# Larger first-batch loads and an earlier third weight product in a fused attention and SwiGLU kernel

## Chip, cores, metric

One core of one Trainium2 chip. The metric is the device time of one execution in microseconds; lower is better. A core's profile gives the span from its first to its last instruction, about 1.8 us less than the time.

## The reference

```python
def _attn_ref(q, k, v, tau):                       # q, k, v: (4, 6016, 256) float32, tau = 1
    qn = q / (np.linalg.norm(q, axis=1, keepdims=True) + 1e-06)
    kn = k / (np.linalg.norm(k, axis=1, keepdims=True) + 1e-06)
    s = kn.transpose(0, 2, 1) @ qn / tau           # 256 x 256 per batch
    s = s - s.max(-1, keepdims=True)
    a = np.exp(s)
    a /= a.sum(-1, keepdims=True) + 1e-09
    return (v @ a).astype(np.float32)

def _moe_ref(x, w_gate, w_val, w_out):             # x: 24064 rows of 256, hidden width 1536
    g = x @ w_gate
    silu = g * (1.0 / (1.0 + np.exp(-g)))
    val = x @ w_val
    return (silu * val @ w_out).astype(np.float32)
```

## The kernel before

The kernel folds the attention matrix into the gate and value weights (the "weight products", `Wg` and `Wv`) and then streams v through the two weighted stages. Batches 1 to 3 do their attention work behind the stream of the batch before. Batch 0 can't: its k and q (47 tiles of 128 rows each, loaded as float32 and cast to fp8 by the DMA) must arrive, be multiplied and normed before the stream starts. That prologue, the first 40 us of some 812, is what the change touches.

Load order and groups (four tiles a load, 4 KB a partition):

```python
groups = [(s, min(4, NS - s)) for s in range(0, NS, 4)]
...                                                            # cut
gs, gm = groups[-1]
qgroups = groups[:-1] + [(s, min(2, NS - s)) for s in range(gs, NS, 2)]
NQ = len(qgroups)
order = [(g, 1, groups) for g in range(NG)] + [(g, 0, qgroups) for g in range(NQ)]
for n, (g, which, gl) in enumerate(order):
    load_qk(0, g, which, gl)                                   # all on the GpSimd queue
    ...                                                        # cut: constants at n == 8
load_first_v()
load_w(0, HW); load_w(HW, WP)                                  # first weight block, in halves
load_v(*allc[1])
for wc in range(1, NWC):
    load_w(wc * WP, (wc + 1) * WP)                             # second weight block first
```

What each group sets off, and the tail:

```python
    sqs = [first_square(0, t, which, on_dve=(t % 2 == 1)) for t in ts]   # ACT and DVE
    if which == 0:
        for t in ts:
            gemm1_pair(0, t)                       # k-times-q products on TensorE, fp8
        if g == G_COLS:                            # from tile 36 on: column sums
            first_cols(0)
    ...                                            # cut: row or column sums of the squares
# tail, in first_softmax(0):
    row_eps(rs)
    transpose_first_v()                            # waits for the first v load
    keep_warm(3)                                   # three 128x512 matmuls on ones
    ...                                            # cut: exponentials on ACT, two halves
    row_sum(0)
    wp_matmul(b, 0, 0, units[0], lo)
    wp_matmul(b, 1, 0, units[1], lo)
    row_sum(1)
    finish_rs(b, rs)
    wp_matmul(b, 0, 1, units[0], lo)
    wp_matmul(b, 1, 1, units[1], lo)
    for u in (2, 3):
        for jh in range(CH):
            wp_matmul(b, u, jh, units[u], lo)
```

`keep_warm` was there before; its name says that it is meant for TensorE's granted clock, the share of its full rate that a throttle lets it run at.

## Time and profile before

| | before |
|---|---|
| time, first three runs | 813.64, 813.80, 814.92; median 813.80 us |
| span of the profiled execution | 811.9 us, mean granted clock 1.000 |
| TensorE busy | 98% of the span |
| first use of q's last tile | 34.37 us |
| TensorE takes over from the loads | 40.60 us |

A row of a timeline reads: start, length, engine, line, operation, output<-inputs, shape, count, and in brackets the idle time before it with what ended it. An engine's line "PEld" is TensorE's weight loads.

### The profile page before, as it was taken

Reading aid. Unit: us, or ns where it says so; the run is one execution under the profiler, and the core shown is the slowest. Engines: PE = TensorE matmul, PEld = TensorE weight load, DVE = VectorE, ACT = ScalarE, POOL = GpSimd, SP = SyncE. Lnnn points to the kernel's source line nnn. Section 1 sums busy time; section 2 is a strip of 40 time slices with the busy share of each in tenths; the row PEclk is TensorE's granted clock in tenths of the full one; section 3 lists DMA queues with packets and bytes.
Section 4 is the critical chain, followed back from the end, with each engine's and each line's share of the span. In section 5 each row is a group of like instructions: output and inputs, shape, how many; then the busy total and the mean of one; then the engine's idle time right before and its main releaser. Section 6 shows DMA issues by size and latency. Waiting matters only on the chain.

```text
span 811.9 us, 13668 instructions
## 1 busy us (share of the span) xinstructions
PE 794.1 (98%) x4952; PEld 488.9 (60%) x5042; DVE 524.3 (65%) x795; ACT 434.8 (54%) x757; POOL 267.2 (33%) x330
## 2 busy tenths in 40 slices
PE   5999999999999999999999999999999999999998
PEld 3656666665565666666565666666556565665666
DVE  4777777657556777656755677765765555555554
ACT  4666655545555556545555556654554544444543
POOL 5515887423000888722100488752300000000000
PEclk9999999999999999999999999999999999999999
DMA  9993875329312678334912377641942112112101
GB/s 87 142 157 69 115 105 86 80 34 150 77 40 46 96 100 106 74 65 95 127 40 59 53 96 112 89 78 37 171 102 66 46 50 55 52 40 65 50 27 59
DMA packets 93747, 64.99 MB, mean 80 GB/s; under 512 B 52896, under 2 KB 92448, under 8 KB 92928
## 3 DMA queue, kind: packets, MB, share of 16 engines
q0 software_dynamic: 19584, 27.41, 29.0%
q1 hardware_dynamic: 73952, 36.65, 18.2%
q8 instruction: 39, 0.64, 0.4%
q14 instruction: 28, 0.23, 0.1%
q10 hardware_dynamic: 144, 0.07, 0.0%
HBM read 79.04 MB, written 36.70 MB: 143 GB/s over the span
## 4 chain that ended last, share of the span: by engine, by line
PE 93%; DMA 4%; issue 1%; DVE 1%; POOL 0%; ACT 0%; POOLq 0%
PE o_new L457 30%; PE v_ps L423 30%; PE g_ps L423 28%; DMA q_sb<-in_q_dram 2%; PE ps L392 2%; PE kq_new L151 2%; DMA k_sb<-in_k_dram 1%; DMA w_gate_sb<-in_moe_w_gate_dram 1%; DVE sv L433 0%; POOL k_sb L106 0%; ACT silu L429 0%; PE last_ps L481 0%; POOL vb L114 0%; DVE sq L274 0%; PE kq_new L156 0%
## 5 line engine op out<-in xcount | busy, mean ns | idle before, releaser
L433 DVE TENSOR_TENSOR sv<-silu,v_ps 128x512 bf16<-128x512 bf16 (+1 forms) x576 | 388.3, 674 | 263.9 <-ACT silu L429 261.1
L429 ACT ACTIVATE silu<-g_ps 128x512 bf16<-128x512 f32 (+1 forms) x576 | 338.7, 588 | 323.4 <-PE g_ps L423 257.5
L457 PE MATMUL o_new<-w_out_sb,sv 128*128 128x256 bf16 x2244 | 337.2, 273 | 1.5
L423 PE MATMUL v_ps<-vT,Wv 128*128 128x512 bf16 (+1 forms) x1100 | 324.3, 374 | 2.9
L423 PE MATMUL g_ps<-vT,Wg 128*128 128x512 bf16 (+1 forms) x1074 | 319.1, 375 | 0.3
L457 PEld LDWEIGHTS <-sv 128*128 128x128 bf16 x2244 | 219.6, 98 | 140.6
L423 PEld LDWEIGHTS <-Wv 128*128 128x128 bf16 x1152 | 112.7, 98 | 130.7
L284 POOL TENSOR_TENSOR acc_new<-acc_new,sq 128x512 f32<-128x512 f32 x135 | 157.6, 1167 | 45.1 <-DVE sq L274 36.9
L423 PEld LDWEIGHTS <-Wg 128*128 128x128 bf16 x1152 | 109.7, 98 | 24.9
L274 DVE TENSOR_TENSOR sq<-q_sb 128x512 bf16<-128x512 fp8e5 x72 | 65.9, 915 | 0.0
L279 POOL TENSOR_TENSOR acc_new<-sq 128x512 f32<-128x512 bf16 x3 | 3.5, 1154 | 150.5 <-DVE sq L274 150.5
L275 ACT ACTIVATE sq<-k_sb 128x512 bf16<-128x512 fp8e5 x72 | 44.2, 614 | 0.0
L466 ACT COPY o_sb<-o_new 128x512 f32<-128x512 f32 x48 | 28.1, 586 | 14.9 <-PE o_new L457 14.5
L151 PE MATMUL kq_new<-k_sb,q_sb 128*128 128x512 fp8e5 x184 | 32.0, 295 | 0.5 <-DMA q_sb<-in_q_dram 0.5
L106 POOL DMA_DIRECT2D q_sb<-in_q_dram x49 | 27.4, 558 | 13.5 <-DMA k_sb<-in_k_dram 5.5
L468 DVE COPY o_sb<-o_new 128x512 f32<-128x512 f32 (+1 forms) x47 | 31.3, 666 | 0.0
L106 POOL DMA_DIRECT2D k_sb<-in_k_dram x48 | 26.0, 542 | 10.4 <-DMA w_out_sb<-in_moe_w_out_dram 5.6
L178 PE MATMUL ss_new<-sq,ones_bf 128*128 128x256 bf16 x83 | 17.8, 353 | 9.1 <-ACT sq L168 8.6
L114 POOL DMA_DIRECT2D vb<-in_v_dram x47 | 24.1, 515 | 5.3 <-DMA vb<-in_v_dram 4.1
L151 PEld LDWEIGHTS <-q_sb 128*128 128x256 fp8e5 x184 | 21.2, 138 | 2.6 <-DMA q_sb<-in_q_dram 2.0
L178 PEld LDWEIGHTS <-ones_bf 128*128 128x128 bf16 x83 | 9.9, 122 | 15.9 <-issue 11.6
L312 POOL TENSOR_TENSOR inv<-inv,half 128x4 f32<-128x4 f32 x3 | 3.1, 1036 | 36.7 <-DVE inv L311 36.7
(94 smaller groups left out, 195.9 us busy)
## 6 DMA issues: line engine op xcount, KB each, us to landing
out_dram<-o_sb SPq DMA_DIRECT2D x92, 256.0 KB, 2.5
vb<-in_v_dram POOLq DMA_DIRECT2D x43, 256.0 KB, 5.9
k_sb<-in_k_dram POOLq DMA_DIRECT2D x44, 128.0 KB, 5.9
q_sb<-in_q_dram POOLq DMA_DIRECT2D x44, 128.0 KB, 5.1
w_out_sb<-in_moe_w_out_dram POOLq DMA_DIRECT2D x1, 768.0 KB, 13.7
vb<-in_v_dram POOLq DMA_DIRECT2D x4, 192.0 KB, 3.5
vT<-vb SPq DMA_TRANSPOSE x47, 4.3
w_gate_sb<-in_moe_w_gate_dram POOLq DMA_DIRECT2D x2, 256.0 KB, 7.0
```

Source lines behind the costliest of these rows:

```text
L106: nc.gpsimd.dma_start(out=dst[:, gs:gs + gm, :], in_=src[b].rearrange("(p s) c -> p s c", s=NS)[:, gs:gs + gm, :])
L151: nc.tensor.matmul(kq[:, jh, :], q_sb[:, ps:ps + 2, js], k_sb[:, ps:ps + 2, :], start=(t == 0 and jh == 0), stop=last, perf_mode=DR, skip_ ...
L178: nc.tensor.matmul(state[b, "ss", which], ones_bf, sq[:, s, :], start=(t == 0 and s == 0), stop=(t == t_last and s == pm - 1))
L274: nc.vector.tensor_mul(sq[:, :pm, 0, :], q_sb[:, ps:ps + pm, :], q_sb[:, ps:ps + pm, :])
L275: nc.scalar.activation(sq[:, :pm, 1, :], k_sb[:, ps:ps + pm, :], ACT.Square)
L284: nc.gpsimd.tensor_tensor(out=acc, in0=acc, in1=sq[:, s, :, :], op=ALU.add)
L423: nc.tensor.matmul(dst[:, :mv], W[:, kk, fs], vT[:, kk, :mv], start=(kk == 0), stop=(kk == CH - 1))
L429: nc.scalar.activation(silu[:, :mv], g_ps[:, :mv], ACT.Silu)
L433: nc.vector.tensor_mul(sv[:, f, :mv], silu[:, :mv], v_ps[:, :mv])
L457: nc.tensor.matmul(self.o_ps[:, j % 2, :], self.sv[:, f, j * P:(j + 1) * P], w_out_sb[:, f, :], start=(f == 0), stop=(f == FH - 1))
L466: nc.scalar.copy(o_sb[:, :m, :], self.o_ps[:, :m, :])
L468: nc.vector.tensor_copy(o_sb[:, :m, :], self.o_ps[:, :m, :])
```

## The change

The intent: fewer and longer loads while the prologue is bound by transfer, and one more weight product that TensorE can do while it waits for the second half of the exponentials.

```diff
         row_sum(0)
         wp_matmul(b, 0, 0, units[0], lo)
         wp_matmul(b, 1, 0, units[1], lo)
+        wp_matmul(b, 2, 0, units[2], lo)
         row_sum(1)
         finish_rs(b, rs)
-        wp_matmul(b, 0, 1, units[0], lo)
-        wp_matmul(b, 1, 1, units[1], lo)
-        for u in (2, 3):
-            for jh in range(CH):
-                wp_matmul(b, u, jh, units[u], lo)
+        for u, jh in ((0, 1), (1, 1), (2, 1), (3, 0), (3, 1)):
+            wp_matmul(b, u, jh, units[u], lo)
...
-    qgroups = groups[:-1] + [(s, min(2, NS - s)) for s in range(gs, NS, 2)]
...
+    kgroups = [(s, min(8, NS - s)) for s in range(0, NS, 8)]
+    qgroups, at = [], 0
+    while at < NS:
+        rest = NS - at
+        size = 8 if rest >= 16 else 4 if rest >= 4 else min(2, rest)
+        qgroups.append((at, size))
+        at += size
+    NG, NQ = len(kgroups), len(qgroups)
+    order = [(g, 1, kgroups) for g in range(NG)] + [(g, 0, qgroups) for g in range(NQ)]
...
-        if n == 8:
+        if n == 4:
```

So k comes in five groups of 8 and one of 7, q in 8, 8, 8, 8, 4, 4, 4, 2, 1. The groups of the later batches stay at four.

More of the change, by code (lines that the diff above doesn't have):

```diff
@@ L529 @@
     VT_AHEAD = 2
-    NG = len(groups)
-    gs, gm = groups[-1]
-    qgroups = groups[:-1] + [(s, min(2, NS - s)) for s in range(gs, NS, 2)]
-    NQ = len(qgroups)
-    order = [(g, 1, groups) for g in range(NG)] + [(g, 0, qgroups) for g in range(NQ)]
+    kgroups = [(s, min(8, NS - s)) for s in range(0, NS, 8)]
[7 more added lines that the diff above has]
+    order = [(g, 1, kgroups) for g in range(NG)] + [(g, 0, qgroups) for g in range(NQ)]
     for n, (g, which, gl) in enumerate(order):
         load_qk(0, g, which, gl)
-        if n == 8:
+        if n == 4:
             make_identity(nc, identf)
```

## The prediction

> **What bounds the kernel now.** I read the page first (shares of the span, the 40 slices, the chain that ended last), then the chain in order of time for the first 70 us, then the engines' busy time in six stretches, then the timelines of the DMA-issuing engine and of TensorE around the places that the diff touches. The page says that TensorE is busy for 98% of the span and makes up 93% of the chain; the 4% that is DMA is all at the start. In order of time that start reads:
>
> ```profile
> 4.56 8.36 DMA k_sb<-in_k_dram
> 12.92 0.28 issue
> 13.21 9.44 DMA q_sb<-in_q_dram
> 22.64 0.28 issue
> 22.93 10.19 DMA q_sb<-in_q_dram
> ...
> 34.03 6.52 DMA w_gate_sb<-in_moe_w_gate_dram
> 40.55 0.04 issue
> 40.60 1.04 PE ps L392 x4
> ```
>
> Columns: start, length, what. From 4.56 to 40.55 us the end hangs on loads: first k and q of batch 0, then the second column block of the weights. At 40.60 TensorE takes over and keeps the chain. The diff touches only what runs before 40.60; the other 771 us can move only by a shift. The stretches show whether the loads are late because they are issued late or because they move bytes all the time:
>
> ```profile
> 4.00:20.00 16.00, 11.40 (x46) 6.34 (x46) 8.06 (x12) 7.55 (x12) 8.62 (x20) 1.00 1.12 104
> 20.00:30.00 10.00, 9.55 (x66) 6.76 (x65) 7.57 (x14) 5.62 (x10) 4.61 (x8) 1.00 1.13 106
> 30.00:34.20 4.20, 3.62 (x41) 2.69 (x39) 2.50 (x5) 2.24 (x4) 2.11 (x4) 1.00 1.15 132
> 40.60:60.00 19.40, 19.29 (x98) 9.81 (x101) 14.11 (x21) 11.69 (x21) 2.65 (x5) 1.00 1.20 162
> ```
>
> (Busy us of PE, PEld, DVE, ACT, POOL, then granted clock, DMA share, GB/s written.) The DMA share is above 1 in every stretch, as packets overlap: the 16 engines never rest. 104 GB/s written in one byte per element is 416 GB/s read in four. No compute engine is full before 20 us. So before 34 us the loads are bound by transfer, not by their issue and not by compute. The issue times say the same:
>
> ```profile
> 15.76 0.53 POOL L106 DMA_DIRECT2D q_sb<-in_q_dram  x1 [0.71 <-DMA k_sb<-in_k_dram]
> 16.97 0.53 POOL L106 DMA_DIRECT2D q_sb<-in_q_dram  x1 [0.68 <-DMA k_sb<-in_k_dram]
> 18.23 0.53 POOL L106 DMA_DIRECT2D q_sb<-in_q_dram  x1 [0.73 <-DMA k_sb<-in_k_dram]
> ...
> 30.50 0.70 POOL L524 DMA_DIRECT2D w_gate_sb<-in_moe_w_gate_dram  x1 [0.53 <-DMA q_sb<-in_q_dram]
> 32.32 0.71 POOL L524 DMA_DIRECT2D w_val_sb<-in_moe_w_val_dram  x1 [1.12 <-DMA q_sb<-in_q_dram]
> ```
>
> Each issue waits until the load eight before it has landed (semaphores 99 to 106, one per load in flight), so the distance of issues is the distance of landings: 8 groups from 8.20 to 18.23 are 10.03 us, 1.254 us for 512 KB. The last line is an exception of 0.55 us, taken up under the rivals.
>
> **What the Trainium skill says.** (1) "DMA: Bandwidth & Descriptors", section "Where 436 GB/s comes from": 16 ports of 32 B at 850 MHz, 27.2 GB/s each. The trace agrees: its packet records give 60, 98, 135 and 173 ns for packets that read 1, 2, 3 and 4 KB, that is 22 ns plus 37.7 ns per KB, and 1024 B in 37.7 ns are 27.2 GB/s. (2) Same page, "Why small descriptors are slow (HBM only)": about 3 cycles of overhead per packet[...]. Below I get 3.3 ns from the trace. (3) Same page, "SWDGE vs HWDGE vs iDMA": a packet is "≤4096 B preferably". If an 8 KB row were cut into two packets, most of the gain would go. The trace speaks against a cut: the v load from DRAM to DRAM, contiguous on both sides, has 16 packets of 16 KB written (32 KB read) at 1226 ns each, and 22 + 32 x 37.7 is 1228. (4) "TensorE: Matmul & The Clock Gate", Part 1: half rate until about 3.4 us of sustained work. In the trace four k-times-q matmuls take 1.15 us at 20.23 and 0.68 us at 21.78, so TensorE turns warm there; I use it in a rival.
>
> **Part 1, the loads.** Tiles stay 47 for k and 47 for q. Before: k in 12 groups (11 of 4, one of 3), q in 13 (11 of 4, then 2 and 1). After: k in 6 (five of 8, one of 7), q in 9 (four of 8, then 4, 4, 4, 2, 1). That is 10 loads fewer, bytes the same, and the last five groups of q (from tile 32) as before; the column-sum stage still begins at tile 36.
> A load puts 8 data packets and one 4-byte semaphore packet (22 ns in the records) on each of the 16 engines. What is not hidden by overlap, x per data packet and y per load, comes from two loads in the trace: with 4 KB rows a packet's share of the period is 1254/8 = 156.7 ns = 150.6 + x + y/8; with the 1 KB rows of the weights (189 packets per half us, so 16 x 500/189 = 42.3 ns, 16 of them per load) it is 42.3 = 37.65 + x + y/16. Hence y is about 22 ns and x about 3.3 ns. Check on the 2 KB rows of the later weight blocks: 75.3 + 3.3 + 1.4 = 80.0 ns, the trace has 97 to 101 per half us, 79 to 82 ns.
> Two groups of 4 cost 2 x 1.254 = 2.508 us. One of 8 costs 8 x (301.2 + 3.3) + 22 ns = 2.458 us. The merge saves 8x + y = 48 ns, and 10 merges save **0.48 us**. The port rate allows no more: 1 MB at 435 GB/s is 2.41 us.
> All ten lie on the chain, ahead of both waits that matter: the landing of q's last tile (TensorE uses it at 34.37) and that of the weight block at 40.55. All loads are in one queue in the same order, so both come 0.48 us earlier. The issues saved on GpSimd (10 x 0.53 us) are worth nothing: it was waiting anyway, and the counts of loads from the tail of q on are the same, so the later issues hang on the same landings.
> Later start of compute: the first load lands after 8 tiles, some 1.25 us later than the 5.47 us at which squares begin now. That is off the chain, because squares of a group of 8 take two ACT and two DVE instructions (2 x 0.63 and 2 x 0.69 us) in a period of 2.46 us.
>
> **Part 2, the third weight product ahead of the second row sum.** It adds and removes nothing; it moves one 128x256 matmul. TensorE now:
>
> ```profile
> 36.48 0.19 PE L246 MATMUL rs<-ones_bf,exT 128*128 128x1 bf16 x2
> 36.53 0.38 PE L392 MATMUL unit_ps<-w_gate_sb,exT 128*128 128x256 bf16 x2
> 36.75 0.19 PE L246 MATMUL rs<-ones_bf,exT 128*128 128x1 bf16 x2
> 36.80 0.38 PE L392 MATMUL unit_ps<-w_gate_sb,exT 128*128 128x256 bf16 x2
> ```
>
> Two products from 36.53 to 36.75 are 0.11 us each, and the row sum follows back to back: the second half of the exponentials (ACT, 35.77 to 36.68) is there just then. There is no gap to fill. The third product pushes the row sum from 36.75 to 36.86, and with it the reciprocal (36.98, 0.17 us) and the first scaled evacuations (37.24). Cost on that branch: **+0.1 us**. But the branch does not set the end:
>
> ```profile
> 39.19 0.59 PE L423 MATMUL g_ps<-vT_new,Wg 128*128 128x512 bf16 x2
> 39.62 0.59 PE L423 MATMUL v_ps<-vT_new,Wv 128*128 128x512 bf16 x2
> 40.60 0.60 PE L392 MATMUL ps<-w_gate_sb,exT 128*128 128x512 bf16 x2 [0.38 <-DMA w_gate_sb<-in_moe_w_gate_dram]
> ```
>
> TensorE waits 0.38 us for the weight block. The 0.1 us goes into this wait; after the change it should be about 0.28 us.
>
> **Sum.** -0.48 us for the loads, 0 for the move (+0.1 hidden): 813.8 - 0.5 = **813.3 us**.
>
> **Rivals.**
> (a) *The rows are cut at 4 KB.* Then only y is saved, 10 x 22 ns = 0.22 us: 813.6. The 32 KB packets speak against it, but they are no casts to fp8.
> (b) *Compute becomes late in the q stage.* A group of 8 needs eight k-times-q matmuls and eight row-sum matmuls, 16 x 0.11 = 1.8 us warm in 2.46 us, but near 4 us if TensorE is still at half rate in the first q group. A lag of about 1 us shrinks by 0.7 us a group and is gone by tile 32. The four square buffers per tensor now hold only one group, so squares wait for the row sums of the group before; at 2.46 us a group that is free. DVE is tightest at tiles 24 to 35: two squares and a reciprocal (0.55 us), then the same on a group of 4, then the row copy. I count it about 0.5 us late at tile 36 and level again by the last tile. Were it not, the q branch would eat the 0.38 us of slack: 813.3 to 814.0.
> (c) *The 0.55 us of lateness before 32.32.* The packet records hold one 16 KB instruction fetch of 944 ns at 29.97 us; the engine that carries it is late with its share, and a load lands with its slowest engine. TensorE's place in its program at 30 us hardly changes, so I expect the same fetch after. Should it fall behind the weight block, another 0.5 us is gained (812.8); should a second one fall into the stage, the gain is gone (813.8).
> (d) *The move of the product pays after all*, if the exponentials end later relative to TensorE than now. It could free 0.1 us on a branch that is hidden anyway: nothing.
>
> **Range and chances.** No path leads to 2% (16 us): all loads of the stage together are some 36 us, transferred at 96% of the port rate. The three runs before span 813.64 to 814.92, so noise is as large as the effect. The centre is 813.3; 812.5 covers the saving plus a fetch out of the way, 814.0 the whole saving lost with some noise. Faster by over 2%: 0.01; within 2%: 0.98; slower: 0.01.
>
> **What would show it.** In the profile after: landings of the groups of 8 at 2.46 us apart (2.51 refutes part 1) and packets of 2 KB written at about 323 ns (173 with twice as many is rival a); the take-over by TensorE at about 40.1 instead of 40.60, still waiting for the weight block; the second row sum after three products, 0.1 us later than its exponentials; TensorE's busy time unchanged from there to the end. I would be wrong if TensorE's wait at the weight block is gone and the chain runs through the squares, or if the take-over moves by more than a microsecond.

## The result, and the profile after

The changed kernel took 814.32 us (median of 6 runs, 813.09 to 816.17) against 814.14 us for the kernel before (6 runs, 813.40 to 814.98). The ratio is 1.0001, 95% interval 0.9986 to 1.0015: the same time. Ratios here are the mean time of one kernel's runs over that of the other's of the same rounds, so not quite the ratio of the medians. The predicted 813.3 (812.5 to 814.0) missed the median.

The six runs are not one cloud: 814.37, 814.37, 814.27 and 816.17 on one side (mean clock 0.994, 0.994, 0.994, 0.992), 813.32 and 813.09 on the other (0.996, 0.999). The profiled execution is one of the first kind (814.37 us, span 812.6). I call an execution above 814.2 us slow in what follows.

The kernel before splits in this round too: 814.92, 814.98 and 814.48 against 813.64, 813.80 and 813.40, three slow of six; the clock of these runs is not on record. So the ratio of 1.0001 compares two mixtures, with four slow of six against three of six. The profile before (813.63 us) is a fast execution, the one after a slow one.

**The loads did what they should.** Stretches of the changed kernel (busy us of PE, PEld, DVE, ACT, POOL, then granted clock, DMA share, GB/s written):

```profile
4.00:20.00 16.00, 9.12 (x44) 5.83 (x44) 7.50 (x12) 6.89 (x12) 5.40 (x14) 0.84 1.06 106
20.00:30.00 10.00, 8.86 (x68) 6.83 (x67) 6.80 (x13) 5.52 (x11) 2.65 (x5) 0.91 1.07 106
34.20:40.60 6.40, 6.23 (x46) 4.15 (x45) 3.69 (x12) 3.58 (x8) 5.05 (x9) 0.73 1.27 203
```

106 GB/s written where it was 104 in the k stage. The load-issuing engine, GpSimd, in the changed kernel:

```profile
26.18 0.73 POOL L522 DMA_DIRECT2D w_gate_sb<-in_moe_w_gate_dram  x1 [1.90 <-DMA q_sb<-in_q_dram]
28.60 0.72 POOL L522 DMA_DIRECT2D w_val_sb<-in_moe_w_val_dram  x1 [1.69 <-DMA q_sb<-in_q_dram]
29.86 0.70 POOL L522 DMA_DIRECT2D w_gate_sb<-in_moe_w_gate_dram  x1 [0.54 <-DMA q_sb<-in_q_dram]
31.16 0.71 POOL L522 DMA_DIRECT2D w_val_sb<-in_moe_w_val_dram  x1 [0.60 <-DMA q_sb<-in_q_dram]
```

The issue that waits for tiles 32 to 35 of q comes at 29.86 instead of 30.50, the one that waits for tiles 36 to 39 at 31.16 instead of 32.32. Between 18.77 and 28.60 four groups of 8 land in 9.83 us, 2.458 us each: the predicted 2.458. The packet records of the first 36 us hold 1280 packets of 2048 B written: 1152 of the groups of 8 at 324 ns (323 was predicted), and 128 of the first v load, which read 4 KB each, at 173 ns. No packet of 4 KB read is left among the groups of 8. So an 8 KB row is one packet.

**But the granted clock in the third stretch is 0.73.** The page's row of TensorE's clock, in tenths, over the first slices of some 20 us each: before, then after.

```profile
PEclk9999999999999999999999999999999999999999
```

```profile
PEclk8899999999999999999999999999999999999999
```

What the tenths hide, the window shows: from 35.42 to 38.83 us, exactly 3.41 us, the changed kernel's TensorE ran at half rate, in the middle of the tail (columns as above):

```profile
35.42:38.83 3.41, 3.41 (x21) 2.04 (x19) 1.71 (x5) 1.68 (x4) 3.40 (x5) 0.50 1.23 206
```

Only 21 matmuls go through in that window; an execution of the same kernel without it has 32. TensorE in the kernel before, then in the changed kernel there:

```profile
35.38 0.62 PE L130 MATMUL vt_ps<-ident,v_sb 128*128 128x128 bf16 x8 [0.17 <-DMA v_sb<-in_v_dram]
...
37.89 0.59 PE L423 MATMUL g_ps<-vT_new,Wg 128*128 128x512 bf16 x2
```

```profile
35.54 1.49 PE L380 MATMUL ps<-warm_bf,ones_bf 128*128 128x512 bf16 x3
...
37.51 0.24 PE L246 MATMUL rs<-ones_bf,exT 128*128 128x1 bf16 x2
...
39.17 0.59 PE L421 MATMUL g_ps<-vT_new,Wg 128*128 128x512 bf16 x2
```

Set against the kernel before: the transposes of v start at 35.03 instead of 35.38 (0.35 us earlier), the second row sum at 37.51 instead of 36.75 (0.76 later), the first gate product at 39.17 instead of 37.89 (1.28 later). TensorE used to be through with what it could do at 40.05 (the last pair before the wait starts at 39.62, and such a pair takes 0.43 us) and to wait for the second weight block until 40.60; now it gets to that point at 41.34 and waits for nothing. 41.34 less 40.60 is 0.74 us, and the profiled times differ by 814.37 - 813.63 = 0.74 us. The account of these two executions closes before 42 us; nothing later matters. The chain that ended last says the same, with TensorE in it from 35.03 on:

```profile
23.74 11.24 DMA v_sb<-in_v_dram
35.03 0.71 PE vt_ps L130 x8
35.75 1.28 PE ps L380 x3
37.06 0.66 PE unit_ps L390 x3
37.75 1.09 PE unit_ps L390 x5
```

**The Trainium skill on this.** "TensorE: Matmul & The Clock Gate", Part 1: a monitor decides in windows of 4096 cycles at 1.2 GHz, 3413 ns, between half and full rate, and the windows run free of the kernel's start. The trace agrees: every stretch of half or full rate in these records, but for the last, which the end of the record cuts, is a multiple of 3.41 us (3.41, 6.83 and 13.65 us in the changed kernel), at another offset in each execution. "Runtime: NRT & Kernel Launch", section "Instruction fetch mechanics": instructions are fetched in 16 KiB blocks of 256. The trace has such packets (16384 B, 945 ns), the first inside the load stage at 30.55 us. The page of the profile counts 39 on their queue, and TensorE's 10084 instructions would be 39.4 blocks (an estimate), so I take them for TensorE's.

### The profile page after: what moved, and what is told of

It is laid out like the page before. It is cut to its first block, busy times and chain, and to the rows that moved or that the text cites. A ratio compares the mean times of both kernels' runs of the same rounds, so it can differ in the third digit from the quotient of the medians.

```text
span 812.6 us, 13747 instructions
## 1 busy us (share of the span) xinstructions
PE 797.2 (98%) x5042; PEld 489.5 (60%) x5042; DVE 524.8 (65%) x795; ACT 434.0 (53%) x757; POOL 262.8 (32%) x320
## 4 chain that ended last, share of the span: by engine, by line
PE 95%; DMA 4%; POOL 1%; issue 0%; DVE 0%; POOLq 0%
PE o_new L455 30%; PE g_ps L421 30%; PE v_ps L421 30%; PE ps L390 2%; DMA q_sb<-in_q_dram 2%; PE kq_new L151 2%; DMA v_sb<-in_v_dram 1%; POOL k_sb L106 0%; PE unit_ps L390 0%; PE last_ps L479 0%; PE ps L380 0%; PE cs L306 0%; PE vt_ps L130 0%; PE kq_new L156 0%; POOL q_sb L106 0%
## 5 line engine op out<-in xcount | busy, mean ns | idle before, releaser
L421 PE MATMUL g_ps<-vT,Wg 128*128 128x512 bf16 (+1 forms) x1128 | 330.7, 375 | 0.0
L421 PE MATMUL v_ps<-vT,Wv 128*128 128x512 bf16 (+1 forms) x1128 | 330.4, 374 | 0.0
L106 POOL DMA_DIRECT2D q_sb<-in_q_dram x45 | 25.3, 562 | 14.7 <-DMA k_sb<-in_k_dram 9.8
L106 POOL DMA_DIRECT2D k_sb<-in_k_dram x42 | 22.8, 544 | 10.6 <-DMA w_out_sb<-in_moe_w_out_dram 4.9
L178 PE MATMUL ss_new<-sq,ones_bf 128*128 128x256 bf16 x83 | 14.8, 336 | 10.9 <-ACT sq L168 10.9
```

Of the source, the lines that this page charges most:

```text
L106: nc.gpsimd.dma_start(out=dst[:, gs:gs + gm, :], in_=src[b].rearrange("(p s) c -> p s c", s=NS)[:, gs:gs + gm, :])
L178: nc.tensor.matmul(state[b, "ss", which], ones_bf, sq[:, s, :], start=(t == 0 and s == 0), stop=(t == t_last and s == pm - 1))
L421: nc.tensor.matmul(dst[:, :mv], W[:, kk, fs], vT[:, kk, :mv], start=(kk == 0), stop=(kk == CH - 1))
```

## The experiments

All runs gave correct results. Times are medians of 5 runs (6 where said) in us; "before" is the kernel before in the same rounds on the same chip. Mean granted clock, known for each execution to 0.001, counts half-rate windows: one of 3.41 us costs 0.5 x 3.41 / 812 = 0.0021. Windows in the k stage count too, and they need cost nothing (an execution of 813.07 us below has 0.995); so a low mean clock is a hint.

### First set: the parts, a second look, and keeping TensorE busy

**The changed kernel, second look** (no edit).

> The changed kernel as it is, a second look. Theory C (clock): the loads do save about 0.4 us, but in some executions TensorE's granted clock falls to half for one window of 3.41 us at about 35.4 us, in the middle of the weight products, and that costs 1.3 us there and 0.7 us net. Then executions of this kernel fall into two groups: those with the half-clock window (about 1 us longer) and those without it (about 0.4 us under the kernel before), and the times go with the mean clock. Rival N (noise): the window is an accident of the profiled run, the times of the runs don't go with the clock, and the mean is that of the kernel before within 0.3 us for another reason.

813.23 us (813.07 to 814.36), before 813.74; ratio 0.9995 (0.9983 to 1.0007). One of five is slow. The profiled execution is a fast one (813.28), with full clock from 18.59 us on and the window that was at half rate above now at full rate:

```profile
35.42:38.83 3.41, 3.41 (x32) 2.19 (x30) 2.46 (x8) 2.74 (x6) 3.37 (x5) 1.00 1.24 207
```

In it TensorE takes over at 40.24 after a wait of 0.40 us for the weight block; 40.1 and 0.28 were predicted. The times do not simply follow the mean clock, though: an execution of 813.07 has 0.995, the slow one of 814.36 has 0.996. In this kernel the clock already rises and falls in the k stage (11.76 to 15.18 full, then half to 18.59), harmlessly.

**The groups of eight alone** (the change without its first hunk).

> The groups of eight alone, with the weight products in their old order. Theory C: as the changed kernel, within 0.2 us: the last q tile some 0.4 us earlier, and the half-clock window at about 35.4 us in most executions, because the loads, not the moved product, take matmuls out of that window. Rival M (the moved product delays the row sum and so the first evacuations, which became the critical path): 0.1 to 0.7 us faster than the changed kernel, and no half-clock window needed for the loss.

814.34 us, before 813.74; ratio 1.0010 (0.9998 to 1.0023); four of five slow. The profiled one (814.52) has half rate from 34.43 to 37.85, and tiles 36 to 39 of q landed late, 2.51 us after the group before them (by the issues that wait for them, 29.99 and 32.50) instead of 1.30 in the changed kernel. The mean clock does not sort these runs: the fast one has 0.996, as the profiled slow one. So the slow executions come without the moved product; rival M is not needed.

**The moved product alone** (the change without its other hunks).

> The third weight product ahead of the second row sum alone, loads in groups of four as before. Theory C: the kernel before within 0.1 us; the second row sum 0.11 us later, TensorE's wait for the second weight block shorter by that; clock at full rate from about 21.7 us. Rival M: 0.1 to 0.7 us slower than the kernel before.

813.81 us (6 runs), before 813.74; ratio 1.0010 (0.9995 to 1.0024), of which one run of 818.11 is most. The second row sum moved to 37.14 with its product ahead of it, TensorE still waited 0.34 us for the weight block (0.27 was expected), full clock from 23.81. The median is as theory C said: nothing. Two of the six are slow, one of them at clock 1.000, so not by a half-rate window.

**Five idle-time matmuls in the tail of the changed kernel.**

```diff
         row_eps(rs)
+        keep_warm(2)
         transpose_first_v()
...
+            if g >= G_COLS:
+                keep_warm(1)
             if g == G_COLS:
                 first_cols(0)
```

> The changed kernel with five idle-time matmuls (128x512 on ones) added on TensorE: one in each of the last groups of q, two before the transposes of v. They do no work for the result. Theory C: the window that ends at about 35.4 us is busy enough, the clock stays full from 22 us on, the first gate product (g_ps) starts at about 37.6 us instead of 39.17, TensorE takes over at about 40.2, and the kernel is 0.3 to 0.5 us faster than the kernel before and about 1 us faster than the changed kernel. Rival N: no faster than the changed kernel, or slower by the 0.2 to 0.6 us that the added matmuls take if they stand on the path.

814.26 us, before 813.74; ratio 1.0001 (0.9989 to 1.0013); three of five slow. The clock was full from 20.73 us as meant, yet the profiled execution is slow (814.26). In it tiles 36 to 39 landed 1.3 us late, and TensorE took over at 41.11 without a wait. That the added matmuls stood on the path is an inference from this, not tested alone. Theory C in its simple form did not explain this execution.

Both profiled slow executions of this set with late tiles had TensorE's 16 KB instruction fetch at 30.19 us, the fast one and the changed kernel's first at 30.51 and 30.55. That made a second theory, F: the fetch delays one DMA engine just as tiles 36 to 39 land, and this makes the slow executions.

### Second set: the tail against the fetch

**Three idle-time matmuls instead of five**, placed where TensorE waits.

```diff
         row_eps(rs)
+        keep_warm(2)
         transpose_first_v()
...
             if g == G_COLS:
+                keep_warm(1)
                 first_cols(0)
```

> The changed kernel with three idle-time matmuls (128x512 on ones) on TensorE: one after the k-times-q products of tiles 36 to 39, while the row copy is awaited, two before the transposes of v, where TensorE waited for the v load. All come after the first instruction fetch of TensorE (30.2 to 30.5 us), so the fetch does not move. Theory C (half-clock window in the softmax tail makes the slow executions, near 814.3): no such window, and nearly all executions near 813.2. Theory F (the 16 KB instruction fetch makes one DMA engine late by 0.6 to 1.3 us just as tiles 36 to 43 of q land; where it hits tiles 36 to 39, the tail is late): slow executions near 814.3 remain as frequent, 2 to 3 of 5.

813.36 us (813.08 to 813.54), before 813.85; ratio 0.9992 (0.9979 to 1.0004). None slow; take-over at 40.17 after a wait of 0.21 us.

**The fetch moved into the k stage.**

```diff
+    pad_ps = psum_o.tile([P, 2, C], FP32, tag="o")
+    for _ in range(100):
+        nc.tensor.matmul(pad_ps[0:1, 0, 0:1], ones_bf[:, 0:1], ones_bf[:, 0:1],
+                         start=True, stop=True)
     for g, which, gl in order:
```

> The changed kernel with 100 one-element matmuls on TensorE ahead of the first row sum, while it has nothing to do (1.7 to some 7 us). They are 200 instructions, so the fetch should fall into the k stage, at about 13 to 17 us instead of 30.4. Theory F: the lateness of one engine moves there too; if it wears off within some loads, q tiles 36 to 43 land on time (about 31.0 and 32.4 us, first use of the last tile about 33.3 instead of 33.9), and executions near 814.3 vanish or get rare; fast ones 812.7 to 813.2. If the engine stays late, no gain over the fast executions of the changed kernel. Theory C: slow executions near 814.3 remain, with a half-clock window near 35 us in them.

813.68 us (813.40 to 813.85), before 813.85; ratio 0.9995. None slow. The first fetch moved to 6.73 us (13 to 17 was expected), and the second load landed some 0.75 us late (from one issue to the next 3.17 us, 6.89 to 10.07, instead of 2.42). That lateness did not wear off: tiles 32 to 35 still came 0.88 us after the changed kernel's, tiles 36 to 39 0.80 us. After a second fetch at 35.26 us TensorE waited 0.57 us for a weight load.

**Both.**

> Both: the 100 early one-element matmuls and the three matmuls of the tail. If C and F are both at work, this alone is free of slow executions: all near 813 or below. If C alone is, it does as the kernel with the three matmuls; if F alone, as the one with the early fetch.

813.67 us (813.41 to 813.82), before 813.85; ratio 0.9996. None slow; as the one above.

**The fetch moved in the kernel before.**

> The kernel before (groups of four) with the 100 early one-element matmuls. Theory F: the 0.55 us of lateness at tiles 36 to 39 is gone or smaller; if the end of the stage hangs on it, 0.3 to 0.6 us faster than the kernel before; if the engine that carries the fetch stays late to the end of its queue, the same time within 0.1 us. Theory C has no say here: the kernel before runs at full clock from some 22 us in all its executions.

813.95 us (813.80 to 815.25), before 813.85; ratio 1.0003. Two of five slow. No gain: TensorE took over at 40.78, after a wait of 0.25 us, so lateness from a fetch at 7.28 us still reaches the weight block, as the second branch of the expectation had it.

### Third set: controls, and the clock provoked

**The groups of eight alone, with the three matmuls.**

> Groups of eight, the weight products in their old order, and the three idle-time matmuls of the tail. Theory C (half-clock window): no slow executions; all between 812.9 and 813.6, 0.4 to 0.5 us under the kernel before. Against the same with the moved product (813.36): equal within 0.15 us, the second row sum about 0.1 us earlier if the move is a delay hidden by the wait for the weight block; 0.2 us or more slower would say that the move pays.

813.78 us (813.16 to 814.98), before 813.76; ratio 1.0000. One slow in spite of the tail matmuls (814.98, clock 0.995), two at 813.8 that nothing here explains; the expectation of five within 813.6 failed. In the profiled execution (813.16) the take-over is at 40.13, against 40.17 with the moved product.

**The kernel before, with the three matmuls.**

> The kernel before with the three idle-time matmuls of the tail. Theory C: it has no half-clock window there to lose, so the same time as before within 0.15 us (or up to 0.2 us more, if they stand on the path); the gain of the changed kernel with them is then the loads' and not theirs. Rival W (the matmuls are worth something in themselves): 0.3 us or more faster.

813.72 us, before 813.76; ratio 0.9999. The added matmuls are worth nothing in themselves.

**The changed kernel, third look** (no edit).

> The changed kernel once more, on the chip of the two above, for the share of slow executions and for one more clock record. Theory C: a mix of executions near 813.2 and near 814.3, as in the two looks before (5 of 11 slow), those near 814.3 with a mean clock of 0.994 to 0.996. Were all five near 813.3, the kernel with the three matmuls would have shown nothing but chance or another chip.

813.31 us (813.07 to 813.55), before 813.76; ratio 0.9994 (0.9981 to 1.0006). None slow. By my own expectation the three matmuls had then shown nothing: five fast executions also come by chance. Over its three looks the changed kernel has 5 slow executions of 16.

**The kernel before with the first v load behind four weight loads.**

```diff
-    load_first_v()
     load_w(0, HW)
     load_w(HW, WP)
+    load_first_v()
```

> The kernel before with the first v load behind the first four weight loads, so that the transposes come some 2.5 us later. TensorE's sparse stretch between the k-times-q products of tiles 36 to 39 (end 32.5) and the matmuls that keep it busy before the row sums (35.4 now) grows from 2.9 to over 5 us, longer than one clock window of 3.41 us, as the changed kernel has 3.6 to 4.0. Theory S (the clock falls when the sparse stretch is longer than a window, whatever the loads are): half-clock windows after 22 us in most executions, mean clock under 0.999, on top of the 1 to 2 us that the late v itself costs. If the clock stays 1.000 in all of them, the groups of eight bring the half clock in some other way.

818.26 us, before 813.76; ratio 1.0052 (1.0040 to 1.0065). The mean clock is 0.996 to 0.998 in all five executions, where the kernel before has 1.000 in nearly all. The profiled one has half rate from 36.92 to 43.74, two windows. The late v cost 4.5 us, not the 1 to 2 expected: the transposes start 2.92 us later (38.30 instead of 35.38), and some 1.6 us is left for the half rate (an estimate). The times go with the clock: 817.24 and 817.85 at 0.998, 818.26 to 818.60 at 0.996. So groups of four lose the clock too when TensorE has little to do for long enough (here idle for 2.90 us before the transposes).

### Fourth set: the fetch nudged by a few instructions

**4 one-element matmuls (8 instructions) at the start of the changed kernel** (the diff of the early fetch with `range(4)`).

> The changed kernel with 4 one-element matmuls (8 instructions) on TensorE at the very start, so the fetch begins some 0.3 to 0.5 us earlier, at 29.8 to 30.1 us. Theory F: tiles 36 to 39 are late (landing near 32.5 instead of 31.2) in all executions, and all five are slow, 814.0 or more. Theory C alone: as the changed kernel, slow in about a third.

813.16 us (813.08 to 813.50), before 813.80; ratio 0.9991 (0.9978 to 1.0003). The fetch fell at 29.65 and tiles 36 to 39 were late, as theory F wanted:

```profile
29.80 0.70 POOL L522 DMA_DIRECT2D w_gate_sb<-in_moe_w_gate_dram  x1 [0.54 <-DMA q_sb<-in_q_dram]
31.96 0.71 POOL L522 DMA_DIRECT2D w_val_sb<-in_moe_w_val_dram  x1 [1.47 <-DMA q_sb<-in_q_dram]
```

2.16 us from issue to issue instead of the changed kernel's 1.30. And none of the five is slow. It has the lowest median of the study.

**10 such matmuls.**

> With 10 such matmuls (20 instructions), the fetch at about 29.3 to 29.6 us. Theory F: it hits the engine before the packets of tiles 36 to 39 too: slow in all executions, by as much or less, as some of the lateness falls on tiles 32 to 35. Theory C alone: slow in about a third.

813.45 us (813.10 to 813.50), before 813.80; ratio 0.9992. Fetch at 28.58, now tiles 32 to 35 late (0.95 us). None slow.

**4 such matmuls and the three of the tail.**

> 4 such matmuls and the three idle-time matmuls of the tail. If the fetch makes the tail late and the half clock does the rest, this has the late tiles but no half clock: 813.4 to 813.9. If the lateness itself is the loss, it stays at 814 or more. If neither, it is near 813.3.

813.53 us (813.47 to 813.66), before 813.80; ratio 0.9995. Late tiles, none slow.

**The fetch later**: row sums of ten k tiles left out. The norm of k is wrong on purpose, though the output still passed the comparison.

```diff
-            else:
+            elif which == 0 or not 1 <= t <= 5:
                 first_row_sums(0, t, which, sq, (T_COLS if which == 0 else NP) - 1)
```

> The changed kernel without the row sums of ten k tiles (20 instructions of TensorE fewer; the result is wrong on purpose in the norm of k), so the fetch begins about 1 us later, at 31.2 to 31.6 us. Theory F: tiles 36 to 39 land on time (31.2) in all executions, and none is slow: all 812.9 to 813.5. Theory C alone: slow in about a third, or more, as TensorE has less to do in the k stage.

814.49 us (813.28 to 814.65), before 813.80; ratio 1.0001. Fetch at 32.10 and tiles 36 to 39 on time in the profiled execution, a fast one, in which TensorE waited 0.81 us for the last three tiles instead; and three of five slow. Theory F does not hold: with 4 one-element matmuls the tiles are late and no execution is slow, and here slow executions remain although the fetch comes behind tiles 36 to 39. And in this kernel the times go with the clock. With twenty instructions less in the k stage, its clock record has no rise and fall there in the profiled execution (full rate from 20.31 to the end). The two fast executions, 813.46 and 813.28, have a mean clock of 1.000, the three slow ones, 814.65, 814.60 and 814.49, have 0.998, which is one window. The difference of the means is 814.58 - 813.37 = 1.21 us. No slow one was profiled, so where its window fell is not on record.

### Fifth set: the same loads with and without 8 instructions

**Groups of eight alone, 4 one-element matmuls.**

> Groups of eight with the weight products in their old order, and 4 one-element matmuls at the start, so that the fetch falls ahead of tiles 36 to 39 and these land near 31.9 instead of 31.2 us. Theory S: the stretch from the end of their products to the keep-warm matmuls is near 3.1 us, under a clock window of 3.41 us: no execution near 814.3, all 813.0 to 813.6. If the half clock or another cause is independent of it: slow ones in a third or more.

813.49 us (813.26 to 813.62), before 813.69; ratio 0.9996. Fetch at 29.51, none slow.

**Groups of eight alone, again, on the same chip.**

> Groups of eight with the weight products in their old order, once more, as the control on the same chip. Theory S: stretch of 4.0 us, slow executions near 814.3 in some (1 to 4 of 5), each with one half-clock window more in its mean clock than the fast ones have. If none is slow, the pair decides nothing.

813.38 us (813.16 to 816.15), before 813.69; ratio 1.0003. Three fast executions at clock 0.998 each, two slow ones (814.04, just under my line, and 816.15) at 0.994 and 0.992: two and three windows more, where one was expected.

### What the sets say together

Call **stretch** the time from the start of the products of tiles 36 to 39 to the first weight load of the keep-warm matmuls; between them TensorE has only the products of the last seven tiles, one-column sums and transposes. The products take some 0.43 us (four at 0.11), so a whole clock window of 3.41 us fits into what follows them if the stretch is over 3.84 us. Kernels without added tail matmuls, one profiled execution for each stretch:

| kernel | stretch, us | slow executions (814.04 counted) |
|---|---|---|
| changed, fetch nudged by 8 | 35.19 - 31.72 = 3.47 | 0 of 5 |
| changed, fetch nudged by 20 | 35.38 - 31.78 = 3.60 | 0 of 5 |
| before | 35.78 - 32.08 = 3.70 | 3 of 47, all three at clock 0.998 |
| changed, fetch early | 35.64 - 31.81 = 3.83 | 0 of 5 |
| loads alone, nudged by 8 | 35.50 - 31.64 = 3.86 | 0 of 5 |
| moved product alone | 36.01 - 32.10 = 3.91 | 2 of 6, one at clock 1.000 |
| before, fetch early | 35.96 - 32.05 = 3.91 | 2 of 5, one at clock 1.000 |
| changed, three looks | 4.45, 4.05, 4.44 | 5 of 16 |
| loads alone, two looks | 4.29, 4.42 | 6 of 10 |
| changed, fetch later | 35.88 - 31.05 = 4.83 | 3 of 5 |
| before, v late | 39.03 - 32.09 = 6.94 | half-rate window in all 5 |

(47 is what the rounds of the experiments hold of the kernel before with a clock record; its three slow of six in the first round are not among them.) A slow execution at clock 1.000 is not explained by a half-rate window.

The table is a pattern, and no proof. Long stretches come with slow executions, but four things speak against the simplest reading, that half rate follows when a whole window fits behind the products:

- 3.86 us is over 3.84 and has none slow; the kernel before is under it and has three.
- If windows run free, a whole one fits into a stretch of 4.4 us in some (4.4 - 3.84)/3.41 = 16% of the executions (an estimate). Slow were 5 of 16 and 6 of 10.
- In the profiled slow execution of the loads alone, the window that ended where half rate began does not lie behind these products. It holds them (columns as above, then TensorE's line):

```profile
31.02:34.43 3.41, 2.51 (x34) 1.96 (x31) 2.22 (x5) 1.79 (x3) 1.59 (x3) 1.00 1.21 155
```

```profile
32.27 0.65 PE L151 MATMUL kq_new<-k_sb,q_sb 128*128 128x512 fp8e5 x4 [0.90 <-DMA q_sb<-in_q_dram]
```

- Outside the first round the changed kernel as it is has 1 slow of 10, the kernel before 3 of 47. That the groups of eight bring slow executions rests on the loads alone (6 of 10) and the later fetch (3 of 5). The nudged changed kernels ran on one chip, the changed kernel as it is on two others.

In the changed kernel (32.01 to 35.42) and with v late (33.50 to 36.92) the window before the fall does lie behind the products. What follows is the likely account, then, and not a shown one.

The fetch matters, but the other way round from theory F: it delays tiles 36 to 39 in the kernel before, so their products come late (32.08), close to the tail, and keep the stretch short. The change brings the tiles forward by half a microsecond and the fetch falls after them (30.55 instead of 29.97). Their products then run at 30.98, 1.10 us earlier, while the tail, which hangs on the last tile and on v, gains only 0.35 us. TensorE's dense work moves away from the tail, and a free-running window can fit between, as it did in the profiled execution.

The fast executions in the third look of the changed kernel, and in the second look of the loads alone, show both parts. Row sums and take-over of the changed kernel:

```profile
36.10 0.19 PE L246 MATMUL rs<-ones_bf,exT 128*128 128x1 bf16 x2
...
36.48 0.19 PE L246 MATMUL rs<-ones_bf,exT 128*128 128x1 bf16 x2
...
40.25 1.04 PE L390 MATMUL ps<-w_gate_sb,exT 128*128 128x512 bf16 x4 [0.41 <-DMA w_gate_sb<-in_moe_w_gate_dram]
```

and of the loads alone:

```profile
35.99 0.19 PE L246 MATMUL rs<-ones_bf,exT 128*128 128x1 bf16 x2
...
36.26 0.20 PE L246 MATMUL rs<-ones_bf,exT 128*128 128x1 bf16 x2
...
40.13 1.04 PE L392 MATMUL ps<-w_gate_sb,exT 128*128 128x512 bf16 x4 [0.39 <-DMA w_gate_sb<-in_moe_w_gate_dram]
```

Row sum to row sum is 0.38 us against 0.27: the moved product delays the second by 0.11. It does not reach the wait for the weight block, which is 0.41 and 0.39: the matmuls before the gate product are the same in another order, and from the start of the transposes to the first gate product it is 2.52 us with the moved product (35.00 to 37.51) and 2.53 without (34.88 to 37.41).

## Why the prediction was right or wrong

- **Size of the loads' saving: right.** Groups of 8 land 2.458 us apart, packets take 324 ns. The eleven fast executions of the changed kernel have a mean of 813.23 us, the 44 fast ones of the kernel before in the rounds of the experiments 813.79. That is 0.56 us, for the 0.48 predicted, over different rounds and chips; no interval of the changed kernel's own comparisons excludes 1.
- **Where the saving arrives: right in the fast executions.** The take-over is at 40.24 and 40.25 instead of 40.60 (0.35 us of the 0.48), and at 40.13 with the loads alone (0.47), still waiting for the weight block. Where the other 0.1 us went is not settled; the start of the first landing differs by up to 0.4 us from execution to execution (the first issue that waits for a landing: 6.81 and 7.19 us in two looks).
- **The move: right that it costs nothing, wrong on where it is hidden.** +0.11 us on the second row sum, as predicted. But it was to eat into the wait for the weight block, from 0.38 to 0.28 us, and that wait is 0.40 and 0.41: the delay is made good before the first gate product.
- **Rival (a), rows cut at 4 KB: did not happen.**
- **The step that failed is the sum, "-0.48 us for the loads, 0 for the move": it has no term for TensorE's clock after 22 us.** Rival (b) asked only whether TensorE would still be at half rate in the first q group, and rival (c) about the fetch closed with "TensorE's place in its program at 30 us hardly changes, so I expect the same fetch after". In the profiled execution TensorE was at half rate from 35.42 to 38.83 us, and took over at 41.34 instead of the predicted 40.1, without a wait. The fetch came 0.57 us later, against tiles that came earlier, and so behind tiles 36 to 39 instead of ahead of them; that this lets the window in is likely, not shown. 5 of 16 executions were slow; one of them was profiled. A slow one costs 1.2 us (measured between fast and slow executions of the kernel with the later fetch; 1.09 us between the two profiled executions of the changed kernel), more than twice the saving. The six runs of the result held four slow ones, hence a median of 814.32.
- **The draw has its share in this.** The other two looks at the same kernel have medians of 813.23 and 813.31, close to the predicted 813.3, and in the first round the kernel before had three slow runs of six as well.
- **"What would show it" caught half of it.** It named as proof of being wrong a vanished wait for the weight block with a chain through the squares. In the profiled execution the wait is gone, but the chain runs from the v load through TensorE; and the take-over moved by 0.74 us, less than the microsecond named.
- **The clock as the cause** is shown for the profiled slow execution of the changed kernel (the account of 0.74 us, and the second look without the window). The six runs of the result and the five with the later fetch are sorted by their mean clock, which supports it. It is not shown for all: one profiled slow execution (five tail matmuls) had full clock and late tiles instead, two executions of other kernels were slow at 1.000, the three slow runs of the kernel before in the first round have no clock on record, and the runs of 816 and 818 us stay unexplained beyond one to three windows in their clock. The threshold in the table is a pattern over fourteen profiled executions, fitted after the fact and then tested on one pair (0 of 5 against 2 of 5). That is weak, and the nudged kernel of the pair came out at 3.86 us, not under the threshold as expected. Why the window falls where it does, and what the monitor counts as busy, is open.

The version with 4 one-element matmuls has the lowest median, 813.16 us against 813.80, but its interval (0.9978 to 1.0003) reaches 1, so no version is shown to beat the kernel before.

## What to carry to other kernels

When a change moves loads by a fraction of a microsecond, ask what else hangs on their times: here the engine with slack lost its clock in some executions, most likely because its dense work moved away from the latency-bound tail. Read the granted clock window by window, not as the mean of the page, and look at the runs one by one, of both kernels, before believing a median of two clusters. A term of 0.5 us that is worked out well is worth little while a state that costs 1.2 us comes and goes with the phase of a window that no one sets.

## What the Trainium skill lacked or had wrong

- "TensorE: Matmul & The Clock Gate", Part 1: its table says that half rate follows an idle window. Here it followed windows that were sparse, not idle: TensorE's matmul records cover 3.01 of the 3.41 us before 35.42 in the changed kernel and 2.51 us before 34.43 in the loads alone. In the kernel with five tail matmuls a window with 2.45 us covered (30.97 to 34.38) kept full rate. The same part tells of falls after short idle times between groups of matmuls, too, but gives no measure of busy that would tell these windows apart.
- "Runtime: NRT & Kernel Launch", section "Instruction fetch mechanics": it calls the cost of a block boundary mostly hidden. No wait of TensorE for instructions shows, but loads landed late with the 16 KB packet (893 to 975 ns): 0.55 us (kernel before, fetch at 29.97), 0.75 us (at 6.73), 0.95 us (at 28.58) and 1.2 us (loads alone, at 30.19). After the fetch at 6.73 tiles 36 to 39 were still 0.80 us late.
- "DMA: Bandwidth & Descriptors", section "SWDGE vs HWDGE vs iDMA": a packet is "≤4096 B preferably". Casting loads with 8 KB rows went as single packets, 324 ns each, 0.02 us less than two of 173 ns; nothing was cut.
- No page: the profile's granted clock reads 1.00 until the first clock record of an execution. In the kernel before, whose first record is at 21.65 us, it shows 1.00 from 4 to 20 us, while four 128x256 row-sum matmuls take 1.01 us there and 0.60 us after 24 us.
